# Batch 0 of a block-sorted attention kernel: the weighted values written transposed, with row sums from a product with ones

## The chip, the cores and the metric

The kernel runs on one core of one Trainium2 chip. The metric is the device time of one launch in microseconds. The kernel before takes 232.64 us (median of three runs, 232.14 to 233.84); the profiled execution spans 229.3 us.

Five engines work side by side, each in the order of its own queue: TensorE (PE, matrix products), VectorE (DVE), ScalarE (ACT), GpSimd (POOL, here mostly the issuer of loads that change the type) and SyncE (SP, the issuer of the other transfers). Products land in PSUM, which DVE and ACT empty into SBUF.

## What is computed

Attention over blocks that a soft permutation has sorted, and then a two-layer feed-forward network:

```python
for _ in range(5):                       # P = sort_net: 4 x 8 heads, 8 x 8 blocks
    P = exp(P - max(P)); P /= sum(P, -1) + 1e-9; P /= sum(P, -2) + 1e-9
k_sorted = einsum('bhij,bhjcd->bhicd', P, k_blocks)      # and the same for v
scores = scale * q_block @ k_sorted_block.T              # per block of 96 tokens
attn = exp(scores - max); attn /= sum(attn, -1)
x = attn @ v_sorted_block                                # (4 * 768) x (8 heads * 64)
h = maximum(x @ w_in, 0)                                 # w_in 512 x 2048
out = (s * h * h + b) @ w_out                            # w_out 2048 x 512
```

There are 4 batches, 8 heads, 768 tokens in 8 blocks of 96, and 64 numbers per head.

## The kernel before

**Stages.** The five softmax rounds of `sort_net` (lines 191 to 208) run at the start on DVE and ACT, while TensorE works on products of zeros (`warm`, line 156: the first argument is how many, the second how many columns each). From there each batch goes through the same pieces: `k_piece` and `v_piece` sort the keys and values by products with the permutation, `q_piece` or `q_blocks` transpose the queries, `s_piece` or `s_banks` make the scores of four blocks and a pair of heads and ACT takes their exponentials into a tile `at`, and the weighted values follow.

**Batches and halves.** A batch is cut into two halves of four blocks (384 tokens). `hp` counts the four pairs of heads. `ffn1(t, ...)` is the first layer for half `t` (0 to 7): eight steps `i`, each of 8 products of 128x384 into a two-bank PSUM tile, a ReLU on ACT (`rt`) and a square on DVE (`gt`). `ffn2(t, ...)` is the second layer. Both take a dictionary of slots: small pieces of other work that are put into the queues after step `i` (or, with the key `("pre", i)`, between the products and the ReLU of step `i`). `ahead=3` means that the products of head pairs 0 and 1 are issued for the first three steps before the other two pairs are needed; the keys -3 to -1 are slots between these.

**Weighted values, batch 0.** `p_piece(b, half, hp)` (line 345) uses the exponentials as the weights of the array, so that the result has tokens on its partitions: `pv`, 96 tokens x (8 groups of 64 values and a sum). The sum is a column of ones that stands beside the values in `VS`. DVE takes the reciprocal of 96x8 sums (line 361) and multiplies (line 362) into `x`. The feed-forward layer needs `x` transposed: for batch 0 `t_piece` (line 367) does it on TensorE in PSUM for two head pairs at a time and has DVE or ACT copy the result to `XT`; for batches 1 to 3 a DMA does it (`t_dma`).

**Buffers.** The PSUM pool `psa` has three buffers of two banks, which rotate over k, v, score, `pv` and first-layer tiles in the order of issue; `psb` has two of one bank. A piece that takes a buffer waits until the work that last used it is done.

**Order.** The queues follow the program's order; nothing is reordered. All loads with a change of type go through POOL's queue in its order: k of batch 0 in three parts, q blocks 0 to 3, then, held back by a small copy on POOL (line 464) that waits for the second key piece, `load_w`: w_in in 14 parts with q blocks 4 to 7 among them, and w_out in 4. `sum_w` and `make_bias` (column sums of w_out, for the term with `b`) lie in slots of `ffn1(1)`.

The order around the change, from line 471 on and in `ffn1(0)` and `ffn1(1)`, is written out by hand:

```python
s_piece(0, 0, 0); s_piece(0, 0, 1); p_piece(0, 0, 0)
s_piece(0, 0, 2); warm(1); p_piece(0, 0, 1)
s_piece(0, 0, 3); warm(1); p_piece(0, 0, 2); warm(1)
t_piece(0, 0, 0, "A"); p_piece(0, 0, 3)
```

Of the kernel before, what the change touches and what calls it, by code (L numbers as in the profile page):

```python
# [9 lines left out]
FP = mybir.dt.float32  # L10
BF = mybir.dt.bfloat16
AF = mybir.ActivationFunctionType
ALU = mybir.AluOpType
# [9 lines left out]
def kernel(  # L23
# [24 lines left out]
    C2 = BLK // 2  # L48
    GAP = 64
    KR = GAP + C2  # L50
    NG = NHP * NB
# [7 lines left out]
    const = ctx.enter_context(tc.tile_pool(name="const", bufs=1))  # L59
# [7 lines left out]
    osb = ctx.enter_context(tc.tile_pool(name="osb", bufs=3))  # L67
    psa = ctx.enter_context(tc.tile_pool(name="psa", bufs=3, space=bass.MemoryType.PSUM))
# [49 lines left out]
    nc.gpsimd.affine_select(out=emat, in_=emat, pattern=[[-H, B], [-1, H], [0, 2 * NB]], base=0,  # L118
                            channel_multiplier=1, compare_op=ALU.not_equal, fill=1.0)
    load("k", 0, 3)  # L120
    load_q(0, range(HB))
    ones = const.tile([128, 32], BF)
    wi = const.tile([128, NHP, d_ff], BF)
    wo = const.tile([128, NF, d_model], BF)
# [1 line left out]
    def load_w():  # L126
        wiv = moe_w_in.rearrange("(a p) f -> p a f", p=128)
        fq = d_ff // 4

        def part(a, f0, f1):  # L130
            nc.gpsimd.dma_start(out=wi[:, a, f0 * fq:f1 * fq], in_=wiv[:, a, f0 * fq:f1 * fq])  # L131

        for a in (0, 1):
            part(a, 0, 2)
        for a in (2, 3):
            part(a, 0, 1)
        load_q(0, range(HB, NB))
        for a in (2, 3):
            part(a, 1, 2)
        for c in (2, 3):  # L140
            for a in range(NHP):
                part(a, c, c + 1)
        wov = moe_w_out.rearrange("(f p) n -> p f n", p=128)
        for c in range(4):
            fs = slice(c * (NF // 4), (c + 1) * (NF // 4))
            nc.gpsimd.dma_start(out=wo[:, fs, :], in_=wov[:, fs, :])  # L146

    def fill_vs(i):
        nc.gpsimd.memset(VS[i][:, :, D:VW], 1.0)
        nc.gpsimd.memset(VS[i][32:GAP, :, D:VW], 0.0)  # L150
        nc.gpsimd.memset(VS[i][32:C2, :, D:VW], 1.0)

    fill_vs(0)
    Z = []

    def warm(n, w=512):
        for _ in range(n):
            if not Z:
                Z.append(psb.tile([128, 512], FP, tag="b", name="z"))
            nc.tensor.matmul(out=Z[0][:, 0:w], lhsT=zeros[:, 0:128], rhs=zeros[:, 0:w],  # L160
                             start=True, stop=True)
# [23 lines left out]
    nc.vector.tensor_tensor(out=sn, in0=sn, in1=rstat.broadcast_to([BH, NB, NB]),  # L185
                            op=ALU.subtract)
    warm(96, 32)
    warm(6)
    warm(122, 64)
    warm(8)  # L190
    for it in range(5):
        nc.scalar.activation(out=sn, in_=sn, func=AF.Exp)
        if it >= 1:
# [49 lines left out]
    def evac(eng, out, in_):  # L243
        if eng == "A":
            nc.scalar.copy(out=out, in_=in_)  # L245
        else:
            nc.vector.tensor_copy(out=out, in_=in_)  # L247
# [63 lines left out]
    AT = {}  # L311
    X = {}
# [51 lines left out]
            in0=pvv[:, :, :, 0:D],  # L364
            in1=rec.unsqueeze(3).broadcast_to([BLK, 2, HB, D]), op=ALU.mult)

    def t_piece(b, half, hp2, eng):

        x = X[b, half]
        if hp2 == 0:  # L370
            XT[b * 2 + half] = xtp.tile([128, HB, NHP, BLK], BF, tag="xt", name="xt")
        tr = psb.tile([128, 1024], BF, tag="b", name="tr")
        for hp in (hp2, hp2 + 1):
            for n in range(HB):
                c0 = (n * 2 + hp % 2) * BLK
                nc.tensor.transpose(out=tr[:, c0:c0 + BLK],
                                    in_=x[:, n, hp * 128:(hp + 1) * 128],
                                    identity=ident[0:BLK, 0:BLK])
        evac(eng, XT[b * 2 + half][:, :, hp2:hp2 + 2, :],
             tr[:, 0:2 * TG].rearrange("p (n a c) -> p n a c", n=HB, a=2))  # L380

    def t_dma(b, half):
        x = X.pop((b, half))
# [87 lines left out]
    v_piece(0, 3 * CK, "D")  # L471
    s_piece(0, 0, 0)
    s_piece(0, 0, 1)
    p_piece(0, 0, 0)
    s_piece(0, 0, 2)
    warm(1)
    p_piece(0, 0, 1)
    s_piece(0, 0, 3)
    warm(1)
    p_piece(0, 0, 2)  # L480
    warm(1)
    Z.clear()
    t_piece(0, 0, 0, "A")
    p_piece(0, 0, 3)

    s_bc = const.tile([128, 1], FP)
    b_bc = const.tile([128, 1], FP)
# [46 lines left out]
    def SC(b, h, i): return lambda: s_piece(b, h, i)  # L534
    def SB(b, h, i): return lambda: s_banks(b, h, i)
    def P(b, h, i): return lambda: p_piece(b, h, i)
    def TP(b, h, i, eng): return lambda: t_piece(b, h, i, eng)
    def TD(b, h): return lambda: t_dma(b, h)
    def PDB(b): return lambda: build_pd(b)
    def QB(b, n0, eng): return lambda: q_blocks(b, n0, eng)  # L540


    ffn1(0, {-2: [TP(0, 0, 2, "D")], ("pre", 1): [QB(0, HB, "D"), QB(0, HB + 2, "D")],
             2: [SB(0, 1, 0)], 3: [SB(0, 1, 1), P(0, 1, 0)], 4: [SB(0, 1, 2), P(0, 1, 1)],
             5: [SB(0, 1, 3), P(0, 1, 2)], 6: [TP(0, 1, 0, "D"), P(0, 1, 3)]}, ahead=3)
    ffn1(1, {-2: [TP(0, 1, 2, "D")], 1: [lambda: take_p(1, B - 1, PB), PDB(1)], 4: [PDB(2)],
             3: [sum_w], 5: [PDB(3), make_bias]}, ahead=3)
    gate = const.tile([128, 1], BF)

    def gated_loads(b):  # L550
# [56 lines left out]
```

The softmax here doesn't subtract the row's maximum and nothing guards it: scores larger than these inputs give would overflow.

## Time and profile before

| stretch, us | what runs | TensorE busy, us | VectorE busy, us |
|---|---|---|---|
| 20.0 to 26.4 | weighted values of half 0, first products of `ffn1(0)` | 4.68 of 6.40 | 4.61 |
| 26.4 to 42.05 | `ffn1(0)` with half 1's scores and weighted values in its slots | 14.98 of 15.65 | 9.44 |
| 42.05 to 53.86 | the rest of `ffn1(1)` | 11.20 of 11.81 | 5.50 |
| 53.86 to 229 | second layer of batch 0, and batches 1 to 3 | 169.08 of 175.14 | 92.65 |

The ends are landmarks of the trace: at 26.4 the last transposed quarter pair of half 0 is in `XT`, at 42.05 that of half 1, at 53.86 the second layer's first product starts. Over the whole span TensorE is busy 218.0 us (95%), DVE 125.3 us (55%), ACT 99.1 us (43%), POOL 67.2 us (29%). "Busy" of TensorE counts products whose modelled ends overlap, so it isn't a measure of how near its peak it runs.

### The profile page before, as it was taken

Reading aid. Unit: us, or ns where it says so; the run is one execution under the profiler, and the core shown is the slowest. Engines: PE = TensorE matmul, PEld = TensorE weight load, DVE = VectorE, ACT = ScalarE, POOL = GpSimd, SP = SyncE. Lnnn points to the kernel's source line nnn. Section 1 sums busy time; section 2 is a strip of 40 time slices with the busy share of each in tenths; the row PEclk is TensorE's granted clock in tenths of the full one; section 3 lists DMA queues with packets and bytes.
Section 4 is the critical chain, followed back from the end, with each engine's and each line's share of the span. In section 5 each row is a group of like instructions: output and inputs, shape, how many; then the busy total and the mean of one; then the engine's idle time right before and its main releaser. Section 6 shows DMA issues by size and latency. Waiting matters only on the chain.

```text
span 229.3 us, 5991 instructions
## 1 busy us (share of the span) xinstructions
PE 218.0 (95%) x2625; PEld 132.0 (58%) x2648; DVE 125.3 (55%) x223; ACT 99.1 (43%) x127; POOL 67.2 (29%) x110
## 2 busy tenths in 40 slices
PE   7997889999899999999999999999999999999993
PEld 5875646545656555666555556555555555654452
DVE  6757466552557544388647634499647534341221
ACT  4957366553433416646334226627152246650000
POOL 8419499344900008392000018291000000000000
PEclk9999999999999999999999999999999999999999
DMA  5997999999991566995111659993112340001212
GB/s 196 211 84 101 167 151 185 211 215 164 103 162 49 117 159 110 189 139 114 51 46 53 149 123 164 175 144 71 49 71 65 121 114 0 3 1 46 93 46 92
DMA packets 53642, 25.82 MB, mean 113 GB/s; under 512 B 44912, under 2 KB 48752, under 8 KB 53616
## 3 DMA queue, kind: packets, MB, share of 16 engines
q0 software_dynamic: 30576, 12.85, 46.4%
q1 hardware_dynamic: 23040, 12.59, 23.4%
q8 instruction: 20, 0.33, 0.6%
q14 instruction: 6, 0.05, 0.1%
HBM read 27.27 MB, written 6.29 MB: 146 GB/s over the span
## 4 chain that ended last, share of the span: by engine, by line
PE 79%; DMA 10%; DVE 4%; POOL 3%; issue 2%; ACT 1%; ACTq 0%; POOLq 0%
PE ops L429 33%; PE hps L404 27%; DMA wo<-in_moe_w_out_dram 6%; PE z L160 5%; DMA qtok<-in_q_dram 4%; DVE gt L419 3%; PE tv L306 3%; PE tp L256 3%; PE pv L356 3%; PE sc L321 2%; POOL wi L131 2%; PE ops L442 2%; POOL wo L146 1%; ACT rt L418 1%; DVE ks L247 1%
## 5 line engine op out<-in xcount | busy, mean ns | idle before, releaser
L404 PE MATMUL hps<-xt,wi 128*128 128x384 bf16 x512 | 85.9, 326 | 1.3 <-ACT xt L245 0.6
L429 PE MATMUL ops<-wo,gt 128*128 128x512 bf16 x348 | 81.4, 379 | 2.3 <-issue 1.9
L418 ACT ACTIVATE rt<-hps 128x768 bf16<-128x768 f32 x64 | 51.1, 811 | 56.9 <-PE hps L404 48.3
L419 DVE TENSOR_TENSOR gt<-rt 128x768 bf16<-128x768 bf16 x64 | 47.6, 750 | 43.7 <-ACT rt L418 42.9
L404 PEld LDWEIGHTS <-wi 128*128 128x128 bf16 x512 | 49.4, 98 | 34.9 <-DMA wi<-in_moe_w_in_dram 1.7
L429 PEld LDWEIGHTS <-gt 128*128 128x128 bf16 x368 | 33.6, 98 | 36.5
L450 DVE SCALAR_TENSOR_TENSOR ot<-ops,s_bc,bias 128x512 f32<-128x512 f32 (+1 forms) x25 | 18.2, 729 | 30.6 <-PE ops L429 28.3
L326 ACT ACTIVATE at<-sc 112x768 bf16<-112x768 f32 x28 | 21.3, 808 | 29.9 <-PE sc L321 29.9
L99 POOL DMA_DIRECT2D qtok<-in_q_dram x32 | 24.9, 791 | 19.3 <-DMA rawv<-in_v_dram 7.8
L362 DVE TENSOR_TENSOR x<-pv,rec 96x512 bf16<-96x512 f32 x32 | 22.0, 687 | 1.1
L247 DVE CAST vs<-tv 112x1024 bf16<-112x1024 f32 x11 | 13.3, 1223 | 10.8 <-PE tv L306 10.7
L170 POOL COPY vp<-rawv 128x384 bf16<-128x384 bf16 x24 | 19.1, 848 | 0.0
L356 PEld LDWEIGHTS <-at 112*128 112x128 bf16 (+1 forms) x256 | 12.8, 101 | 7.2 <-ACT at L326 1.1
L553 POOL COPY gate<-gt 128x1 bf16<-128x1 bf16 x2 | 0.4, 192 | 55.6 <-DVE gt L419 55.6
L356 PE MATMUL pv<-vs,at 112*128 112x66 bf16 (+1 forms) x256 | 13.9, 195 | 1.1 <-DVE vs L247 1.0
L160 PE MATMUL z<-zeros 128*128 128x64 bf16 (+2 forms) x235 | 12.3, 213 | 1.3 <-DVE zeros L102 1.0
L306 PEld LDWEIGHTS <-vp 128*64 128x64 bf16 x512 | 9.1, 113 | 3.9 <-issue 3.3
L306 PE MATMUL tv<-pd,vp 128*64 128x64 bf16 x512 | 10.2, 197 | 0.9 <-issue 0.7
L160 PEld LDWEIGHTS <-zeros 128*128 128x128 bf16 x238 | 8.6, 104 | 3.7 <-issue 1.7
L245 ACT CAST ks<-tp 128x1024 bf16<-128x1024 f32 x8 | 8.0, 1018 | 3.9 <-PE tp L256 3.9
L245 ACT CAST vs<-tv 112x1024 bf16<-112x1024 f32 x5 | 5.1, 1019 | 9.9 <-PE tv L306 9.9
L361 DVE RECIPROCAL rec<-pv 96x8 f32<-96x8 f32 x32 | 6.4, 200 | 4.9 <-PE pv L356 4.9
(77 smaller groups left out, 105.8 us busy)
## 6 DMA issues: line engine op xcount, KB each, us to landing
out_dram<-ot SPq DMA_DIRECT2D x23, 256.0 KB, 2.0
qtok<-in_q_dram POOLq DMA_DIRECT2D x32, 96.0 KB, 9.5
rawk<-in_k_dram POOLq DMA_DIRECT2D x3, 768.0 KB, 7.9
rawv<-in_v_dram POOLq DMA_DIRECT2D x3, 768.0 KB, 10.8
wo<-in_moe_w_out_dram POOLq DMA_DIRECT2D x4, 512.0 KB, 11.3
v0f<-in_v_dram SPq DMA_DIRECT2D x4, 384.0 KB, 4.8
wi<-in_moe_w_in_dram POOLq DMA_DIRECT2D x12, 128.0 KB, 5.8
rawk<-in_k_dram POOLq DMA_DIRECT2D x3, 256.0 KB, 8.1
```

The lines of the kernel that those rows point to most:

```text
L99: nc.gpsimd.dma_start(out=QTOK[b][:, n], in_=qv[:, n])
L160: nc.tensor.matmul(out=Z[0][:, 0:w], lhsT=zeros[:, 0:128], rhs=zeros[:, 0:w], start=True, stop=True)
L170: eng.tensor_copy(out=o, in_=i)
L306: nc.tensor.matmul(out=ps[z * GAP:(z + 1) * GAP, d, :], lhsT=VP[b % 2][:, d0 + d, :], rhs=PD[b][:, :, z, :], start=True, stop=True)
L326: nc.scalar.activation(out=at, in_=sc[0:KR, :, 0:TG], func=AF.Exp, scale=scale)
L356: nc.tensor.matmul(out=pv[0:m, e, n * VW:(n + 1) * VW], lhsT=atf[:, c0:c0 + m], rhs=VS[b % 2][:, e * NG + g0 + n, :], start=True, stop=True)
L362: nc.vector.tensor_tensor(out=x[:, :, hp * 128:(hp + 1) * 128].rearrange("p n (e d) -> p e n d", e=2), in0=pvv[:, :, :, 0:D], in1=rec.unsq ...
L404: nc.tensor.matmul(out=H1[i][:, f, 0:TG], lhsT=wi[:, hp, fc:fc + 128], rhs=xt[:, :, hp, :], start=(hp == 0), stop=(hp == NHP - 1))
L418: nc.scalar.activation(out=rt, in_=h, func=AF.Relu)
L419: nc.vector.tensor_tensor(out=gt[:, 2 * i:2 * i + 2, :], in0=rt, in1=rt, op=ALU.mult)
L429: nc.tensor.matmul(out=ops, lhsT=gt[:, f, m * 128:(m + 1) * 128], rhs=wo[:, f, :], start=(f == 0), stop=(f == NF - 1))
L450: nc.vector.scalar_tensor_tensor(out=ot[:, ns], in0=ops, scalar=s_bc, in1=BIAS[0][:, ns], op0=ALU.mult, op1=ALU.add)
```

## The change

For batch 0 the weighted values come out already transposed. `pt_piece` takes the place of `p_piece` and `t_piece`: the sorted values are the weights of the array and the exponentials stream past them, so the result has the 128 numbers of a head pair on its partitions and 384 tokens along the row, as `XT` wants it. The sums over keys are then needed on every one of the 128 partitions: two more products, with a matrix of ones (`rsum`, with zeros in the rows of the gap) in the place of the values, write them as a tile `ps` of 128x384. DVE takes the reciprocal of that tile into `rec` and multiplies it with `pv` into `XT`. The transposes, their copies and the tile `x` fall away for batch 0.

Beside that: the w_in loads of the first half of its columns go in quarters (512 columns each) for all four row groups, in place of two halves and four quarters; q blocks 4 and 5 are loaded with 0 to 3, ahead of the copy that holds back `load_w`, and 6 and 7 stay in it; three products of zeros between the pieces go, and the ones of the start are 3 wide, 125 narrow and 10 wide in place of 6, 122 and 8; `ffn1(1)` no longer issues its products ahead; `sum_w` moves from step 3 to step 5 and `make_bias` from 5 to 7.

```diff
-    load_q(0, range(HB))
+    load_q(0, range(HB + 2))
...
-        for a in (0, 1):
-            part(a, 0, 2)
-        for a in (2, 3):
-            part(a, 0, 1)
-        load_q(0, range(HB, NB))
-        for a in (2, 3):
-            part(a, 1, 2)
+        for c in (0, 1):
+            for a in (0, 1):
+                part(a, c, c + 1)
+        for c in (0, 1):
+            for a in (2, 3):
+                part(a, c, c + 1)
+            if c == 0:
+                load_q(0, range(HB + 2, NB))
...
+    rsum = const.tile([KR, D], BF)
+    nc.gpsimd.memset(rsum, 1.0)
+    nc.gpsimd.memset(rsum[32:GAP], 0.0)
+    nc.gpsimd.memset(rsum[32:C2], 1.0)
...
-    warm(6)
-    warm(122, 64)
-    warm(8)
+    warm(3)
+    warm(125, 64)
+    warm(10)
...
-    def t_piece(b, half, hp2, eng):
...
+    def pt_piece(b, half, hp, own=False):
+        g0 = hp * NB + half * HB
+        at = AT.pop((b, half, hp))
+        if hp == 0:
+            XT[b * 2 + half] = xtp.tile([128, HB, NHP, BLK], BF, tag="xt", name="xt")
+        if own:
+            pv, ps = [psb.tile([128, TG], FP, tag="b", name="ptb") for _ in range(2)]
+        else:
+            pt = psa.tile([128, 2, 512], FP, tag="a", name="pt")
+            pv, ps = pt[:, 0, 0:TG], pt[:, 1, 0:TG]
+        for n in range(HB):
+            for e in range(2):
+                nc.tensor.matmul(out=pv[e * 64:(e + 1) * 64, n * BLK:(n + 1) * BLK],
+                                 lhsT=VS[b % 2][:, e * NG + g0 + n, 0:D],
+                                 rhs=at[:, e, n * BLK:(n + 1) * BLK], start=True, stop=True)
+        for e in range(2):
+            nc.tensor.matmul(out=ps[e * 64:(e + 1) * 64, :], lhsT=rsum, rhs=at[:, e, :],
+                             start=True, stop=True)
+        rec = osb.tile([128, d_model], FP, tag="ot", name="rect")[:, 0:TG]
+        nc.vector.reciprocal(out=rec, in_=ps)
+        nc.vector.tensor_tensor(out=XT[b * 2 + half][:, :, hp, :],
+                                in0=pv.rearrange("p (n t) -> p n t", n=HB),
+                                in1=rec.rearrange("p (n t) -> p n t", n=HB), op=ALU.mult)
...
-    p_piece(0, 0, 0)
+    pt_piece(0, 0, 0)
     s_piece(0, 0, 2)
     warm(1)
-    p_piece(0, 0, 1)
+    pt_piece(0, 0, 1)
     s_piece(0, 0, 3)
-    warm(1)
-    p_piece(0, 0, 2)
-    warm(1)
     Z.clear()
-    t_piece(0, 0, 0, "A")
-    p_piece(0, 0, 3)
+    pt_piece(0, 0, 2)
...
-    ffn1(0, {-2: [TP(0, 0, 2, "D")], ("pre", 1): [QB(0, HB, "D"), QB(0, HB + 2, "D")],
-             2: [SB(0, 1, 0)], 3: [SB(0, 1, 1), P(0, 1, 0)], 4: [SB(0, 1, 2), P(0, 1, 1)],
-             5: [SB(0, 1, 3), P(0, 1, 2)], 6: [TP(0, 1, 0, "D"), P(0, 1, 3)]}, ahead=3)
-    ffn1(1, {-2: [TP(0, 1, 2, "D")], 1: [lambda: take_p(1, B - 1, PB), PDB(1)], 4: [PDB(2)],
-             3: [sum_w], 5: [PDB(3), make_bias]}, ahead=3)
+    ffn1(0, {-2: [PTP(0, 0, 3, True)],
+             ("pre", 1): [QB(0, HB, "D"), QB(0, HB + 2, "D")],
+             2: [SB(0, 1, 0)], 3: [SB(0, 1, 1), PTP(0, 1, 0)], 4: [SB(0, 1, 2), PTP(0, 1, 1)],
+             5: [SB(0, 1, 3), PTP(0, 1, 2)], 6: [PTP(0, 1, 3)]}, ahead=3)
+    ffn1(1, {1: [lambda: take_p(1, B - 1, PB), PDB(1)], 4: [PDB(2)], 5: [PDB(3), sum_w],
+             7: [make_bias]})
```

More of the change, by code (lines that the diff above doesn't have):

```diff
@@ L365, in p_piece @@
             in1=rec.unsqueeze(3).broadcast_to([BLK, 2, HB, D]), op=ALU.mult)
-    def t_piece(b, half, hp2, eng):
-        x = X[b, half]
-        if hp2 == 0:
+    def pt_piece(b, half, hp, own=False):
+        g0 = hp * NB + half * HB
+        at = AT.pop((b, half, hp))
+        if hp == 0:
             XT[b * 2 + half] = xtp.tile([128, HB, NHP, BLK], BF, tag="xt", name="xt")
[L372 to L380, printed above, removed]
+        if own:
[16 more added lines that the diff above has]
+                                in1=rec.rearrange("p (n t) -> p n t", n=HB), op=ALU.mult)
     def t_dma(b, half):
@@ L536, in P, with PTP @@
     def P(b, h, i): return lambda: p_piece(b, h, i)
-    def TP(b, h, i, eng): return lambda: t_piece(b, h, i, eng)
+    def PTP(b, h, i, own=False): return lambda: pt_piece(b, h, i, own)
     def TD(b, h): return lambda: t_dma(b, h)
```

## The prediction

> **What bounds the kernel now.** I read the page's busy shares first, then the chain of work that ended last, then the shapes on VectorE, then the timeline of 20 to 54 us, where all the edits lie.
>
> ```profile
> PE 218.0 (95%) x2625; PEld 132.0 (58%) x2648; DVE 125.3 (55%) x223; ACT 99.1 (43%) x127; POOL 67.2 (29%) x110
> ...
> PE 79%; DMA 10%; DVE 4%; POOL 3%; issue 2%; ACT 1%; ACTq 0%; POOLq 0%
> ```
>
> TensorE sets the time; VectorE holds 4% of the chain. But these are averages. The chain in order of time shows that the start is another regime:
>
> ```profile
> 10.31 1.67 PE z L160 x7
> 11.99 1.03 PE pe L219 x8
> ...
> 19.72 8.14 DMA qtok<-in_q_dram
> 27.86 0.28 issue
> ...
> 33.06 14.14 DMA wo<-in_moe_w_out_dram
> 47.21 0.04 issue
> ...
> 53.86 2.54 PE ops L429 x11
> ```
>
> Products of zeros hold up the permutation at 11.99; then come the q and w_out loads; from 53.86 on nearly all is TensorE. So 53.86 (the first second-layer product) is the landmark: what follows is 175 us of work that the change doesn't touch, and moves as one piece.
>
> VectorE's forms, with the time of one:
>
> ```profile
> L450 DVE SCALAR_TENSOR_TENSOR ot<-ops,s_bc,bias 128x512 f32<-128x512 f32 x23 | 17.3, 751 | 28.3 <-PE ops L429 28.3
> L362 DVE TENSOR_TENSOR x<-pv,rec 96x512 bf16<-96x512 f32 x32 | 22.0, 687 | 1.1
> L361 DVE RECIPROCAL rec<-pv 96x8 f32<-96x8 f32 x32 | 6.4, 200 | 4.9 <-PE pv L356 4.9
> ...
> L450 DVE SCALAR_TENSOR_TENSOR ot<-ops,s_bc,bias 128x256 f32<-128x256 f32 x2 | 1.0, 484 | 2.3 <-PE ops L442 2.3
> L198 DVE RECIPROCAL rrec<-rstat 32x8 f32<-32x8 f32 x5 | 1.0, 191 | 0.2
> ...
> L233 DVE RECIPROCAL RC<-cs 128x3 f32<-128x3 f32 x1 | 0.2, 176 | 0.0
> L233 DVE RECIPROCAL RC<-cs 128x1 f32<-128x1 f32 x1 | 0.2, 165 | 0.0
> ```
>
> An ordinary operation costs (751-484)/256 = 1.04 ns for each element of a row. The reciprocal is dearer: from 1 to 3 elements on 128 partitions it grows by 11 ns, 5.5 ns each; from 3 to the 8 of L361, 24 ns, 4.8 each. Today its rows are 8 long, so this is hidden in the fixed 160 ns. The change makes them 384 long.
>
> **What the Trainium skill says.** "VectorE: DVE Perf Modes", section "First, the fixed hardware budget": the reciprocal is an iterative divide with a repeat count of 8, unlike the one-slice operations. The trace agrees that it is several times dearer per element, but shows about 5 cycles at the page's 0.96 GHz, not 8. The same page, "Why PSUM operands drop a tier": fp32 from PSUM runs at one element a cycle; the 1.04 ns agree. "TensorE: Matmul & The Clock Gate", section "What's actually happening": TensorE runs at half rate until it has been busy for a window of about 3.4 us, and falls back after an idle one. The trace agrees at the start: weight loads of the first wide zero products stand 0.43 us apart, the last seven take 0.24 each.
>
> **The change part by part.**
>
> *Reciprocal.* 160 + 384 x 5.4 = 2.23 us, once for each of 8 pieces. Bounds: 0.56 us if long rows ran at 1.04 ns; 1.3 to 1.6 if the slope were 3.0 (128x3 to 32x8) or 3.7 (128x1 to 32x8), which mix partition counts; 0.15 + 384 x 8/0.96 = 3.36 us, an estimate from the page's repeat count. I take 2.23, since 128x1, 128x3 and 96x8 lie on one line.
>
> *Multiply.* 128x384 from PSUM: 687 - 128 x 1.04 = 0.55 us. With gaps of 0.03 between VectorE instructions a piece costs it 2.84 us. Before, it costs 0.20 + 0.69 us and half a copy of 0.55 (one of the four copies is ACT's): 8 x 0.89 + 3 x 0.55 = 8.8 us in all. After: 22.7. VectorE gains 13.9 us of work, mostly between 20 and 42, where it has 6.40-4.61 + 15.65-9.44 = 8.0 us idle. That alone forces about 6 us; the order of dependences adds to it.
>
> *TensorE.* Removed: 8 x 0.43 (L356) and 4 x 0.51 (transposes) = 5.5 us. Added: per piece 8 products of 96 columns (as a score piece, 0.34) and two of 384 (0.16 each) = 0.66, so 5.3. Nothing either way.
>
> *Half 0.* The first weighted values come at 20.8, the first reciprocal at about 21.5 (0.25 later than the 21.25 of before, for the longer piece). VectorE then runs the four pieces back to back: 21.5 + 4 x 2.84 = 32.9 for head pair 3 of half 0. Before, this stands at 26.37:
>
> ```profile
> 25.81 0.56 DVE L247 COPY xt<-tr 128x768 bf16<-128x768 bf16 x1 [0.84 <-PE tr L376]
> 27.76 1.51 ACT L418 ACTIVATE rt<-hps 128x768 bf16<-128x768 f32 x2 [3.19 <-PE hps L404]
> ```
>
> The fourth score piece also waits for the first multiply, which frees its PSUM buffer (24.3, before 22.24), but its exponential (done by 25.7) is ready well ahead of its turn on VectorE. First-layer products of pairs 0 and 1 for three steps (2 us) go in the meantime; then TensorE stands until 32.9. First ReLU at 33.5, 5.7 later. The q blocks and w_in that before arrive at 28 to 30 are then long there.
>
> *Half 1.* In steps 3 to 6 VectorE has to do a square (0.56), a reciprocal and a multiply in each: 3.43 us with gaps. TensorE's pace before is 1.95:
>
> ```profile
> 32.86 1.47 PE L404 MATMUL hps<-xt,wi 128*128 128x384 bf16 x8
> ...
> 34.81 1.47 PE L404 MATMUL hps<-xt,wi 128*128 128x384 bf16 x8
> ...
> 36.77 1.47 PE L404 MATMUL hps<-xt,wi 128*128 128x384 bf16 x8
> ```
>
> Three PSUM buffers rotate between first-layer tiles and pieces, so step i+2 waits for the multiply of the piece of step i: TensorE falls to VectorE's pace. From 33.5, steps 0 to 3 with the q blocks take till 38.8 (before: 27.76 to 33.7, part of it a wait for w_in that is now gone). Then 38.8 + 2.84 + 3 x 3.43 = 51.9 for the last multiply into half 1's `XT`. Before: 42.05.
>
> *`ffn1(1)`.* Its first step needs all four pairs, so no product beyond the first three gets past 51.9; the missing `ahead` costs little beside that. Then 61 products at 20.80/128 = 0.1625 us (a later stretch of the chain) = 9.9, the sums of w_out 16 products in 1.1, the bias 0.86: 63.8, against 53.86. All of w_out is there by 47.2 in the trace of before, so the wait of 0.85 us inside those sums is gone, and moving them later costs nothing. Sum so far: +9.9.
>
> *Zeros at the start.* Three wide ones at 0.43 fewer, two more at 0.24, three more narrow ones; the clock turns at about 7 us in both (narrow ones 36 ns each before it, 21 after): 5.25 + 49 x 0.036 + 76 x 0.021 + 10 x 0.24 = 11.0 in place of 11.98. The permutation is ready at 11.07, so its products go 0.75 us earlier than 11.91, and so does all of the above. -0.75.
>
> *Loads.* The two q blocks follow q 0 to 3 in a gap (32 GB/s in 14 to 16 us, 8 in 16 to 18), w_in's first quarters come a little sooner: hidden behind VectorE now. The three fills of `rsum` on POOL lie in its 8 us of waiting before line 464. Batch 1's k and v loads have 9 us more, so TensorE's wait for the value copy on POOL (0.42 at 60.66) goes: about -0.4. The dropped three zero products lie in what is now idle.
>
> Sum: 232.64 + 9.9 - 0.75 - 0.4 = **241.4 us**.
>
> **The rivals.**
> A. *Long rows at full rate* (0.56 us): a piece costs VectorE 1.17, half 0 is ready near 26.7, half 1 near 41.2, no load is waited for, and the second layer starts about 1 us sooner; with the zeros and POOL's wait, 230.5. For it: the removed transposes and waits for q and w_in (1.4 and 1.7 us of POOL, 0.6 and 1.7 of TensorE). Against: three sizes show 5 ns an element.
> B. *A middle slope* (1.3 to 1.6 us): half 1 ready at 44.6 to 46.5, second layer at 56.5 to 58: +2.6 to +4.1, less 1.15: 234 to 235.6. For it: the 32x8 form at 191. Against: it has 32 partitions; a sum over 64 elements takes 207 ns there and 220 on 128.
> C. *Eight cycles an element*, 3.36 us: half 1 at 61, second layer at 73, 250.5. For it: the page's count. Against: 8.3 ns would put 128x3 at 182, not 176.
> D. *TensorE goes cold* in the idle of 22 to 33 us: its products slow to half for a few us. For it: it works about half of that time and stands 2 us at once. Against: no gap reaches 3.4 us, and VectorE, not it, is awaited. Up to +2 on the forecast: 243.5.
>
> **How the numbers follow.** Forecast with D's share: 0.72; A 0.10; B 0.10; C 0.08. The forecast's own spread: slope 5 to 6 ns gives reciprocals of 2.08 to 2.46, that is about -1.2 and +1.8 (eight of them, nearly all exposed), and D to 245 on top. Range 235 to 245.5: holds the forecast and the upper end of B, leaves out A, C and the rest of B. Faster is A, 0.10; slower the forecast, C and nearly all of B, 0.88; same 0.02.
>
> **What would show it.** Right: reciprocals of 128x384 near 2.2 us, 18 us in all; VectorE nearly full from 21 to 52; the chain in that stretch on the reciprocal line, not q and w_out loads; first-layer products waiting for VectorE; the second layer's first product at about 63; the stretch after it as long as before. Wrong: reciprocals under 1 us (A), or a wait of TensorE for loads before 50.

## The result: 14 us slower, and the profile after

The changed kernel takes 247.08 us (median of four runs, 245.12 to 251.60) against 233.02 us of the kernel before; the ratio is 1.0576, 95% interval 1.0491 to 1.0662. The direction and the main mechanism, VectorE's long reciprocals, were forecast (241.4 us, range 235 to 245.5), but the time lies above the range. One thing has to be known to read the times below: the granted TensorE clock differs from run to run of one kernel (0.945 to 0.970 over these four), a run in which it falls longer takes longer, and the ratios leave out runs more than 1.5% above the fastest.

The page of the changed kernel, busy shares and chain by engine, then the granted clock in 40 slices of 6.1 us each; the last line is the clock of the kernel before, in slices of 5.7 us:

```profile
PE 225.4 (93%) x2632; PEld 132.7 (55%) x2632; DVE 143.2 (59%) x220; ACT 98.5 (40%) x126; POOL 69.4 (29%) x115
...
PE 85%; DVE 12%; ACT 1%; issue 1%
...
PEclk9999579997999999999999999999999999999999
```

```profile
PEclk9999999999999999999999999999999999999999
```

VectorE has 17.9 us more to do (143.2 against 125.3) and holds 12% of the chain against 4%. The waits for q and w_out are gone from the chain. New is the fall of the clock: before, the row is all nines; here it is lower in slices 5, 6 and 10.

The chain of waits of the changed kernel in order of time (start, length, what) shows where the 14 us are:

```profile
18.52 0.94 issue
...
21.62 2.57 DVE rect L393
...
24.21 0.56 DVE xt L394
24.77 2.48 DVE rect L393
...
33.38 0.57 DVE xt L394
...
33.99 2.18 PE hps L420 x7
36.17 1.28 PE tqb L293 x16
...
50.95 0.56 DVE xt L394
51.50 0.47 DVE gt L435
51.97 2.48 DVE rect L393
...
54.47 0.57 DVE xt L394
...
55.08 8.97 PE hps L420 x45
64.05 0.98 PE cps L534 x16
```

From 21.62 to 33.95 and from 40.83 to 55.04 the chain runs through VectorE: reciprocal, multiply, next reciprocal, and in half 1 a square between. Between the halves it runs for 6.0 us through TensorE (first-layer products, the q transposes and a score piece) and 0.8 through a ReLU. The last multiply ends at 55.03, where before the last copy into half 1's `XT` ended at 42.05; the second layer begins at 68.43, before at 53.86. The two lines of the timelines, the copy before and the second layer's first products after:

```profile
41.50 0.55 DVE L247 COPY xt<-tr 128x768 bf16<-128x768 bf16 x1
```

```profile
68.43 2.75 PE L445 MATMUL ops<-wo,gt 128*128 128x512 bf16 x12
```

After that nothing has changed: 243.3 - 68.43 = 174.9 us to the end, before 229.3 - 53.86 = 175.4.

VectorE's two new forms (count, busy us, mean ns):

```profile
L393 DVE RECIPROCAL rect<-pt 128x384 f32<-128x384 f32 x7 | 17.9, 2551 | 0.6 <-PE pt L390 0.6
...
L394 DVE TENSOR_TENSOR xt<-pt,rect 128x384 bf16<-128x384 f32 x7 | 3.9, 557 | 0.2
L393 DVE RECIPROCAL rect<-ptb 128x384 f32<-128x384 f32 x1 | 2.5, 2548 | 0.0
```

The multiply is the 0.55 us of the forecast. The reciprocal is 2.55 us, not 2.23.

The stages of the kernels below are compared by these landmarks, read in each timeline (us):

| kernel | first reciprocal of batch 0's values | last write into half 1's `XT` ends | second layer begins | from there to the end |
|---|---|---|---|---|
| before | 21.25 | 42.05 | 53.86 | 175.4 |
| after | 21.62 | 55.03 | 68.43 | 174.9 |
| forecast for after | 20.75 | 51.15 | 63.05 | 175.0 |
| e2_busy | 22.38 | 55.69 | 70.41 | 174.5 |
| e10_form (copies) | | 40.09 | 51.99 | 174.9 |
| e13_after (after again) | 24.29 | 57.61 | 72.37 | 174.7 |
| e14_same (TensorE kept busy) | 24.37 | 56.99 | 68.90 | 174.9 |
| e15_stream (before, short stream) | 20.25 | 40.55 | 52.00 | 175.4 |
| e16_stream_after | 21.92 | 54.16 | 68.92 | 174.9 |
| e17_stream_busy | 20.13 | 52.74 | 64.64 | 174.5 |

The forecast's row takes its 0.75 us for the zero products off its 21.5, 51.9 and 63.8. The last column is the same for all to 0.9 us: nearly all that differs lies before it.

### The profile page after: what moved, and what is told of

Same layout as the page of the kernel before. It is cut to its first block, busy times and chain, and to the rows that moved or that the text cites. A ratio compares the mean times of both kernels' runs of the same rounds, so it can differ in the third digit from the quotient of the medians.

```text
span 243.3 us, 5981 instructions
## 1 busy us (share of the span) xinstructions
PE 225.4 (93%) x2632; PEld 132.7 (55%) x2632; DVE 143.2 (59%) x220; ACT 98.5 (40%) x126; POOL 69.4 (29%) x115
## 3 DMA queue, kind: packets, MB, share of 16 engines
HBM read 27.27 MB, written 6.29 MB: 138 GB/s over the span
## 4 chain that ended last, share of the span: by engine, by line
PE 85%; DVE 12%; ACT 1%; issue 1%
PE ops L445 33%; PE hps L420 32%; DVE rect L393 8%; PE z L165 5%; PE tv L311 4%; PE pv L361 3%; PE tp L261 2%; PE sc L326 2%; DVE xt L394 2%; PE ops L458 1%; DVE gt L435 1%; PE tqb L293 1%; DVE vs L252 1%; PE pe L224 0%; ACT ks L250 0%
## 5 line engine op out<-in xcount | busy, mean ns | idle before, releaser
L420 PE MATMUL hps<-xt,wi 128*128 128x384 bf16 x512 | 89.9, 335 | 9.5 <-DVE xt L394 8.3
L445 PE MATMUL ops<-wo,gt 128*128 128x512 bf16 x368 | 85.7, 380 | 0.0
L420 PEld LDWEIGHTS <-wi 128*128 128x128 bf16 x512 | 50.5, 100 | 46.9 <-issue 15.6
L435 DVE TENSOR_TENSOR gt<-rt 128x768 bf16<-128x768 bf16 x64 | 49.0, 774 | 40.0 <-ACT rt L434 39.4
L175 POOL COPY vp<-rawv 128x384 bf16<-128x384 bf16 x24 | 19.9, 881 | 0.0
L393 DVE RECIPROCAL rect<-pt 128x384 f32<-128x384 f32 x7 | 17.9, 2551 | 0.6 <-PE pt L390 0.6
L367 DVE TENSOR_TENSOR x<-pv,rec 96x512 bf16<-96x512 f32 x24 | 16.5, 686 | 0.8
L361 PEld LDWEIGHTS <-at 112*128 112x128 bf16 x192 | 9.9, 101 | 5.7
L361 PE MATMUL pv<-vs,at 112*128 112x66 bf16 x192 | 10.4, 195 | 0.0
L131 POOL DMA_DIRECT2D wi<-in_moe_w_in_dram x16 | 8.6, 553 | 2.6 <-DMA wi<-in_moe_w_in_dram 1.8
```

Of the source, the lines that this page charges most:

```text
L175: eng.tensor_copy(out=o, in_=i)
L361: nc.tensor.matmul(out=pv[0:m, e, n * VW:(n + 1) * VW], lhsT=atf[:, c0:c0 + m], rhs=VS[b % 2][:, e * NG + g0 + n, :], start=True, stop=True)
L393: nc.vector.reciprocal(out=rec, in_=ps)
L420: nc.tensor.matmul(out=H1[i][:, f, 0:TG], lhsT=wi[:, hp, fc:fc + 128], rhs=xt[:, :, hp, :], start=(hp == 0), stop=(hp == NHP - 1))
L435: nc.vector.tensor_tensor(out=gt[:, 2 * i:2 * i + 2, :], in0=rt, in1=rt, op=ALU.mult)
L445: nc.tensor.matmul(out=ops, lhsT=gt[:, f, m * 128:(m + 1) * 128], rhs=wo[:, f, :], start=(f == 0), stop=(f == NF - 1))
```

## Experiments

### Is it the reciprocal?

**e1_copy.** A copy in its place.

```diff
-        nc.vector.reciprocal(out=rec, in_=ps)
+        nc.vector.tensor_copy(out=rec, in_=ps)
```

> The changed kernel with the eight reciprocals of 128x384 turned into plain copies of the sums, so the weighted values are multiplied by their sums and not divided: this part of the computation is left out. A copy of 128x384 fp32 from PSUM should take 0.55 us against the 2.55 us that the reciprocal takes in the profile after. Theory (the long-row reciprocals on VectorE are the cause, and TensorE's lowered clock follows from the idle that they make): eight times 2.0 us leave VectorE, half 0 is ready near 26.5, half 1 near 41.5, the granted clock is back at 0.99 or more, and the whole takes 230 to 234 us. Rival (the missing products ahead of the second half, the other form of the products and the new order of loads carry a good part): it stays at 237 to 243 us.

Measured: 234.21 us, ratio to before 1.0103 (1.0041 to 1.0165), granted clock 0.976 to 0.991. Copies took 0.55 us each. So 4.7 of the 5.8% hang on the length of that one instruction, as the theory has it (6.6 of 7.6 with the changed kernel's later ratio, e13_after); but the clock did not come back, and 234.21 is just above the theory's range. Something besides the reciprocal was left: in its profile the first copy began at 24.88, behind two waits in TensorE's stream of 2.13 and 1.20 us, which are taken up below.

**e3_recip.** The other direction: the kernel before, with an idle reciprocal added to each of the eight pieces (`bias` is filled with ones early, and gets its value later as ever).

```diff
         nc.vector.reciprocal(out=rec, in_=pvv[:, :, :, D])
+        if b == 0:
+            nc.vector.reciprocal(out=bias[:, 0:TG], in_=bias[:, 0:TG])
```

> The kernel before with one idle reciprocal of 128x384 fp32 (on a constant in SBUF) put between the small reciprocal and the multiply of each of the eight weighted-values pieces of batch 0; nothing else changes. Theory (VectorE's added time alone makes the loss): each takes 2.5 us, a piece costs VectorE 3.4 us, half 0 is ready about 10 us later and half 1's pieces come every 4 us in place of 2: 243 to 249 us, as slow as the changed kernel or slower. Rival (VectorE has 8 us to spare between 20 and 42 us and the pieces are not awaited at once): 233 to 238 us.

Measured: 248.30 us, ratio 1.0757 (1.0695 to 1.0819), clock 0.950 to 0.965. None of the change's other parts is in it, and it is as slow as the change. The rival, room on VectorE, falls.

**e9_half.** Half of the columns.

```diff
-        nc.vector.reciprocal(out=rec, in_=ps)
+        nc.vector.reciprocal(out=rec[:, 0:TG // 2], in_=ps[:, 0:TG // 2])
...
-                                in1=rec.rearrange("p (n t) -> p n t", n=HB), op=ALU.mult)
+            in1=spread(rec, [[0, 2], [BLK, 2], [1, BLK]]), op=ALU.mult)
```

> The changed kernel with the reciprocal taken of half of the columns only: 128x192 in place of 128x384, used twice, so that the second half of the tokens is divided by the sums of the first: this part of the computation is changed. By the measured sizes it takes 1.35 us in place of 2.55. Theory (the reciprocals are exposed nearly whole, and the loss is linear in their length): eight times 1.2 us less, 9.6 us, and a little more from the clock: about 237 to 239 us, close to the middle between the changed kernel (247) and the one with copies (234 on its chip, 3 us over the kernel before). Rival (the clock and TensorE's fetch waits carry most of it, so that it falls in a step and not in proportion): 241 us or more, or already at 234.

Measured: 236.68 us, ratio 1.0267 (1.0212 to 1.0322), clock 0.971 to 0.976. This is 0.3 us under the theory's range. The ratios of the three lengths (0.55, 1.35 and 2.55 us of VectorE) are 1.010, 1.027 and 1.058, but they come from different chips, and the changed kernel alone gave 1.058 and, repeated, 1.076 (e13_after). The profiles show the shape better. From the first reciprocal or copy to the last multiply it takes 18.8 us in e10_form (copies, below), 22.9 in e9 and 33.4 in the changed kernel: the first 8 x 0.8 = 6.4 us of VectorE's time cost 4.0, the next 9.6 cost 10.5, of which 1.2 are the clock between the halves. So there is no step, but a bend, not a line: the shorter pieces still find part of VectorE's idle time, and from half length on nearly all of it is exposed.

### Why was the reciprocal mis-sized?

**e5_sizes.** Many lengths, after the last store of the kernel before.

```diff
+    for parts in (128, 32):
+        for n in (1, 3, 8, 16, 48, 96, 192, 384):
+            nc.vector.reciprocal(out=w[0:parts, 0:n], in_=w[0:parts, 0:n])
...
+    for n in (8, 96, 384):
+        nc.vector.reciprocal(out=w[:, 0:n], in_=ps[:, 0, 0:n])
```

> The kernel before with reciprocals of many row lengths added after its last store: 1, 3, 8, 16, 48, 96, 192 and 384 fp32 elements on 128 and on 32 partitions in SBUF, and 8, 96 and 384 on 128 partitions from PSUM. Theory (the cost is a fixed part and one slope over all lengths, and the forecast's 5.4 ns an element was read too low from rows of 1 to 8): the slope is (2551 - 165)/383 = 6.2 ns at 96 and more, the same on 32 and 128 partitions and from PSUM and SBUF. Rival (the slope of short rows, 5.4 ns, is right there, and PSUM or the partition count makes long rows dearer): 384 in SBUF takes 2.2 us.

Its VectorE groups by shape; the mean time of one in ns stands after the comma:

```profile
L585 DVE RECIPROCAL bias<-psx 128x384 f32<-128x384 f32 x1 | 2.6, 2557 | 0.0
L581 DVE RECIPROCAL bias<-bias 128x384 f32<-128x384 f32 x1 | 2.6, 2553 | 0.0
L581 DVE RECIPROCAL bias<-bias 32x384 f32<-32x384 f32 x1 | 2.5, 2541 | 0.0
...
L581 DVE RECIPROCAL bias<-bias 128x96 f32<-128x96 f32 x1 | 0.8, 753 | 0.0
...
L581 DVE RECIPROCAL bias<-bias 128x16 f32<-128x16 f32 x1 | 0.3, 253 | 0.0
...
L581 DVE RECIPROCAL bias<-bias 128x8 f32<-128x8 f32 x1 | 0.2, 203 | 0.0
...
L581 DVE RECIPROCAL bias<-bias 128x3 f32<-128x3 f32 x1 | 0.2, 175 | 0.0
```

From 8 elements on the slope is (2553-203)/376 = 6.25 ns; from 3 to 8 it is (203-175)/5 = 5.6. 128 partitions in place of 32 add 12 ns from 3 elements on, and PSUM 3 to 4, whatever the length. Theory: right. The forecast's 5.4 came from rows too short to show the slope, and mixed 96 with 128 partitions. Its rival C, eight cycles, would be 8.3 ns; at the 0.96 GHz that the Trainium skill gives ("VectorE: DVE Perf Modes", section "Specifications") 6.25 ns are six.

### What the small parts of the change do

**e4_small** put all of them into the kernel before; **e6_sixq** the q blocks alone, **e7_zeros** the zero products alone, **e11_rest** all but the q blocks. **e8_fourq** took the q blocks out of the changed kernel.

```diff
e4, e6         -    load_q(0, range(HB))
e4, e6         +    load_q(0, range(HB + 2))
e4, e7, e11    -    warm(6)
e4, e7, e11    -    warm(122, 64)
e4, e7, e11    -    warm(8)
e4, e7, e11    +    warm(3)
e4, e7, e11    +    warm(125, 64)
e4, e7, e11    +    warm(10)
e4, e11        w_in in quarters; sum_w in step 5, make_bias in step 7
e8             -    load_q(0, range(HB + 2))
e8             +    load_q(0, range(HB))
```

> The kernel before with only the small parts of the change: six q blocks ahead of the held-back loads, w_in in quarters, 3 wide, 125 narrow and 10 wide zero products at the start, column sums in step 5 and the bias in step 7 of the second half. The weighted values stay as they were, and so do the products issued ahead. Theory (these parts are neutral or help a little): TensorE no longer waits for q and w_in at 28 to 30 us, 231 to 232.5 us. Rival (in the changed kernel a part of the loss comes from them): 234 to 236 us.

> The kernel before with only the q blocks moved: six in place of four ahead of the held-back loads, two within them. Theory (the two more blocks keep the transfer engines full to about 15.3 us in place of 14.2, and TensorE's instruction fetches, which lie in the same stretch, come late: in the kernel with the small parts together TensorE stood 1.65 us at 15.5 and 2.13 us at 20.1 for nothing that the profile shows): two such waits of 1 to 2 us here too, a lower clock after them, 233.5 to 236 us. Rival (the other small parts, above all the zero products, bring the waits and the clock): 230.5 to 232 us, as before.

> The kernel before with only the zero products of the start changed: 3 wide, 125 narrow and 10 wide. Theory (they are shorter by 0.2 to 0.8 us and leave the clock as it is): 230 to 231.5 us. Rival (fewer wide products at the start leave the clock nearer to falling, and it falls between 20 and 34 us): 233 us or more, with a granted clock under 0.99.

> The kernel before with the small parts except the q blocks: w_in in quarters, the shorter zero products, sums in steps 5 and 7. Theory (each is neutral or helps, and only the q blocks did harm): 229.5 to 230.8 us, a little under the kernel before. Rival (the quarters, with two more loads in the held-back series, also delay something): 231.5 us or more.

> The changed kernel with four q blocks ahead of the held-back loads, as in the kernel before, and four within them; the rest of the change stays. Theory (the late instruction fetches belong to the two q blocks and cost the changed kernel 1 to 3 us): 243 to 245.5 us against 247, the first long reciprocal at 21.2 us or sooner. Rival (VectorE's reciprocals hide whatever TensorE loses ahead of them, or the fetches have nothing to do with q): 246 to 248 us.

Measured: e4 235.55 us, ratio 1.0160 (1.0106 to 1.0214), where the theory had 231 to 232.5; e6 235.64 us, of which three runs took 235.2 to 238.3 at a clock of 0.964 to 0.978 (the ratio of 1.0234, 1.0111 to 1.0356, is that of these three) and one 230.1 at a clock of 1.0, no more than the kernel before; e7 230.97 us, 0.9975 (0.9948 to 1.0001); e11 231.15 us, 1.0025 (1.0002 to 1.0048); e8 247.64 us, 1.0632 (1.0463 to 1.0801).

The rest of the small parts is neutral, and e11's expected gain did not show. With the two q blocks ahead a run at a lower clock is likelier in the kernel before: a clock of 0.985 or less stood in all six runs of e4 and three of four of e6, against five of 20 in e7 and four of 22 in e11. Those are few runs, and where the clock holds no loss is shown. In the changed kernel taking the q blocks back helped nothing. So they are not the cause of the mishap; at most they make it likelier.

The mishap itself is a wait in TensorE's timeline. First e4_small, then the kernel before, the products of the value pieces (in brackets the idle time ahead and what ended it):

```profile
15.15 0.35 PE L307 MATMUL tv<-pd,vp 128*64 128x64 bf16 x10
17.14 1.04 PE L307 MATMUL tv<-pd,vp 128*64 128x64 bf16 x54 [1.65 <-issue]
...
19.00 1.11 PE L307 MATMUL tv<-pd,vp 128*64 128x64 bf16 x58
22.24 0.28 PE L307 MATMUL tv<-pd,vp 128*64 128x64 bf16 x6 [2.13 <-issue]
```

```profile
17.63 1.14 PE L306 MATMUL tv<-pd,vp 128*64 128x64 bf16 x60
19.12 0.25 PE L306 MATMUL tv<-pd,vp 128*64 128x64 bf16 x4 [0.35 <-issue]
```

"issue" is time in which nothing that the profile shows was awaited. Sixteen profiles have that start with its narrow products. In twelve there is a wait at both places, 10 to 12 products into the first value piece and 4 to 6 before the end of the fourth; in the other four (both of the first comparison, e3 and e10) only the second. They last 0.35 to 2.7 us: 0.94 us in the first profile of the changed kernel, and 4.5 us in two parts in that of e8. What they bring about is seen in e4: the window of 3.4 us with the second wait has TensorE busy for only 1.2 us, and from 23.1 us on the clock is half for 10.2 us.

**e15_stream.** Do the waits belong to the work, or to the place in the stream of instructions?

```diff
     warm(6)
-    warm(122, 64)
+    warm(12)
     warm(8)
```

> The kernel before with the 122 narrow zero products of the start replaced by 12 wide ones, which take about as long: 110 products and as many weight loads fewer ahead of the key and value pieces, and nothing else. TensorE's two waits for nothing that the profile shows stand at the 11th product of the first value piece and near the end of the fourth in every kernel so far. Theory (they belong to places in TensorE's instruction stream, where the next stretch of instructions is fetched, and not to the work there): both move about 110 products later, the first into the fourth value piece, the second beyond the scores into the first layer, and the runs vary less. Rival (they belong to the work or to the time, such as buffers or the transfers of q): they stay at the same products or the same microseconds.

Measured: 229.48 us, ratio 0.9955 (0.9936 to 0.9973), the 22 runs between 228.32 and 230.72 us at a clock of 0.991 to 1.0. Its value products:

```profile
14.91 1.42 PE L306 MATMUL tv<-pd,vp 128*64 128x64 bf16 x64
...
17.05 1.32 PE L306 MATMUL tv<-pd,vp 128*64 128x64 bf16 x64
```

Both waits are gone from the value pieces, and the first reciprocal comes at 20.25. They did not turn up 110 products later either, so neither theory nor rival came out as written.

Two things in the kept traces settle what the waits are. First, their places are counted in products: with 6 + 122 + 8 = 136 zero products ahead they stand 12 products into the first piece and 4 before the end, with 3 + 125 + 10 = 138 two products earlier (10 and 6), and from one to the other there are 128 products, each with its weight load (52 + 16 + 60 or 54 + 16 + 58). Second, the DMA part of the page has a queue of kind "instruction" with 20 packets, and in the packed traces these are 16384 bytes each. All 28 waits in the value pieces end 1.25 to 1.62 us after the end of one of these packets; in e4 they end at 15.88 and 20.71, and TensorE goes on at 17.14 and 22.24. So these are late fetches of instructions.

In e15 the packet ends at 16.32. By the count, the place that it serves lies 110 products later, near 17.9 us (an estimate from the count and the 1.32 us of the last 64 products): 1.6 us after the packet, and no wait is left. Twelve wide products take about as long as 122 narrow ones but are far fewer instructions. What makes a packet come late stays open: the second one starts between 13.0 and 15.4 us in these sixteen profiles, with four q blocks (e11, 15.4) as with six (the changed kernel, 13.0). This version is 0.45% under the kernel before.

### What the clock costs

**e2_busy** and **e12_allbusy** give TensorE something to do where it stands for VectorE: e2 repeats products of two pieces, e12 also puts wide zero products ahead of the third first-layer tile and of the second half.

```diff
e2, e12   -    pt_piece(0, 0, 2)
e2, e12   +    pt_piece(0, 0, 2, times=5)
e2, e12   -    ffn1(0, {-2: [PTP(0, 0, 3, True)],
e2, e12   +    ffn1(0, {-2: [PTP(0, 0, 3, True, 3)],
...
e12       +            if t == 0 and i == ahead - 1:
e12       +                H1[i] = psa.tile([128, 2, 512], FP, tag="a", name="hps")
e12       +                for _ in range(12):
e12       +                    nc.tensor.matmul(out=H1[i][:, 0, :], lhsT=zeros[:, 0:128],
e12       +                                     rhs=zeros, start=True, stop=True)
...
e12       +             7: [Z.clear, lambda: warm(16)]}, ahead=3)
```

> The changed kernel with the products of the third weighted-values piece issued five times and those of the fourth three times, each time with the same result in the same place, so that TensorE works in the time in which it stood from 24.8 to 27.9 and from 29 to 31 us. Theory (the lowered clock between 24 and 36 us is an effect of its own, which costs the seven products of 2.18 us at 34 us and the sixteen transposes of 1.28 us about 1.7 us): these run at full rate, the second layer starts 1.5 to 2 us earlier, 243 to 245.5 us against 247. Rival (the clock is not set by this idle, or VectorE is awaited in any case): 246 to 249 us with the same granted clock.

> The changed kernel with TensorE kept busy in all three places where it stood for VectorE: the repeated products of the third and fourth piece, twelve wide zero products ahead of the third first-layer tile (30 to 33 us), and sixteen ahead of the second half's first product (50 to 54 us). VectorE's work is the same. Theory (TensorE's lowered clock is a loss of its own only where TensorE is awaited, above all in the products after 55 us: 45 of them took 8.97 us and not 7.3): the granted clock is 0.985 or more, 243.5 to 245.5 us against 247. Rival (the clock costs nothing, since VectorE is awaited throughout): 247 us with the better clock too.

Measured: e2 248.43 us, 1.0719 (1.0657 to 1.0781). The clock held until 34.2 us, then was half to 37.6 and again from 54.7 to 61.5 us: the low stretches moved and the time did not gain. Here the theory failed. e12: 244.01 us, 1.0580 (1.0520 to 1.0639), with the same ratio as the first runs of the changed kernel, on another occasion: unclear. So both were put side by side, e14_same being the kernel of e12.

> The changed kernel itself again, on one chip with the kernel whose TensorE is kept busy. Theory (5 us of the loss beyond the forecast are the longer reciprocal, 2.6 us, the clock after 55 us, 1.5 us, and TensorE's waits near 15 and 20 us, which differ from run to run): 245 to 248 us, with a granted clock of 0.96 to 0.975. Rival (the first runs were an unlucky draw): 242 to 244 us.

> The changed kernel with TensorE kept busy while VectorE is awaited, now beside the changed kernel on one chip. Theory (the clock costs something of its own in the products after the last multiply): 1 to 2.5 us under the changed kernel, and the same 11.9 us from the end of the last multiply to the second layer where the changed kernel has 13.4. Rival (the clock's loss is hidden behind VectorE): less than 0.7 us apart.

Measured: e13 248.51 us, ratio 1.0760 (1.0701 to 1.0818); e14 246.75 us (one run of 241.66 at a clock of 0.998, five of 245.5 to 247.2 at 0.971 to 0.979; no ratio). So one and the same kernel gave 1.0576 and 1.0760 on two occasions, and ratios of different experiments can be held against each other to about 2% only. The repeated run of the changed kernel was slower than the first: its first reciprocal came at 24.29. The medians differ by 1.8 us; plainer is the landmark: from the last multiply to the second layer 14.8 us in e13 and 11.9 in e14. The theory's 13.4 for the changed kernel was that of its first profile; the clock takes different stretches in different runs. e14's own first reciprocal is late for the same reason as e13's, waits of 2.25 and 0.56 us in the stream.

The last pair took the waits in the stream away from the changed kernel (e16), and the idle of TensorE too (e17).

```diff
e16, e17  -    warm(125, 64)
e16, e17  +    warm(13)
e17       and the edits of e12
```

> The changed kernel with its 125 narrow zero products of the start replaced by 13 wide ones, so that the stream ahead of the key and value pieces is 112 products shorter, as in the kernel that did away with TensorE's waits near 15 and 20 us. Theory (these waits cost the changed kernel what its first long reciprocal comes late: 24.29 us in its second profile, 21.62 in its first, against 20.6 without them): first reciprocal at 20.6, last multiply ended 33.4 later at 54.0, second layer 13.4 later at 67.4, and 174.7 to the end: a span of 242 and a time of 243.5 to 244.5 us, with less spread. Rival (VectorE's chain or the clock takes back what the start gains): 246 us or more.

> The same stream, and TensorE kept busy in the three places where it stands for VectorE. Theory (with the waits of the start gone and the clock kept, only the reciprocals are left of the loss): second layer 11.9 us after the last multiply and not 13.4, 241.5 to 243 us, granted clock 0.99 or more, at least 1 us under the kernel with the shorter stream alone. Rival (the clock is hidden behind VectorE): the two within 0.7 us.

Measured: e16 243.87 us, ratio 1.0538 (1.0473 to 1.0602); e17 241.21 us, 1.0452 (1.0403 to 1.0502), clock 0.986 to 1.0. The last stretch of e17's chain, to be held against the changed kernel's (8.97 us for the same 45 products):

```profile
52.18 0.57 DVE xt L395
52.75 0.04 issue
52.79 7.47 PE hps L421 x45
60.26 0.98 PE cps L540 x16
61.24 2.71 PE hps L421 x16
```

7.47 and not 8.97 us: 1.5 us of the changed kernel's loss in its first profile are clock, where TensorE is awaited; in e13 the same 45 products took 10.33, 2.9 us more than in e17. Between e16 and e17 lie 2.7 us of the medians, more than the 1 us that the theory asked for.

e16's time is as expected; its first reciprocal, expected at 20.6, came at 21.92 in the execution profiled, the slowest of the six, and e17's at 20.13. No wait in the stream made it late: ScalarE, in the order of its queue, stood 1.97 us for a load of v until 10.64, and with it the last softmax round that the permutation needs. So a late load at the start is one more thing that differs from run to run.

### Is the new form worth anything?

**e10_form.** The new form with a cheap stand-in for the reciprocal and none of the small load and zero-product parts (the order of w_in and the zero products go back too; not printed).

```diff
-    load_q(0, range(HB + 2))
+    load_q(0, range(HB))
...
-        nc.vector.reciprocal(out=rec, in_=ps)
+        nc.vector.tensor_copy(out=rec, in_=ps)
```

> The kernel before with only the new form of the weighted values (transposed, the product with ones, no products ahead in the second half, sums in steps 5 and 7), the reciprocal turned into a copy (that part of the computation is left out), and the q blocks, the order of w_in and the zero products as before. Theory (the form with a cheap reciprocal would be worth 1 to 2 us, and what held the kernel with copies at 234 us were the q blocks and what they do to TensorE's fetches and clock): 229 to 231 us. Rival (the form is worth nothing even with a free reciprocal): 231.5 to 234 us.

Measured: 230.17 us, ratio 0.9961 (0.9936 to 0.9986). With a division that cost no more than a copy the form would gain 0.4%. In the profiled execution, the fastest of the 20, the second layer begins at 51.99, 1.9 us earlier than in the first profile of the kernel before.

## Why the prediction was right, and where it was wrong

Its working, against the first profile of the changed kernel, whose span of 243.3 us is 5.25 over the forecast's 229.3 + 8.75 = 238.05:

- **Reciprocal (the step that failed first).** "160 + 384 x 5.4 = 2.23 us" measured 2.55: the slope is 6.25 ns, and the spread given, 2.08 to 2.46, did not reach it. The three sizes that it calls one line (165, 176 and 200 ns at 1, 3 and 8 elements) give 5.0 from end to end, still further off. Of the 8 x 0.32 = 2.6 us some was given back, since a reciprocal starts about 0.08 us before the recorded end of the multiply ahead, where 0.03 of gap was assumed. A piece of half 0 costs 3.06 us, not 2.84 (multiplies at 24.21 and 27.27), one of half 1 3.52, not 3.43 (43.90 and 47.42). Half 0 took 12.3 us (forecast 11.4), half 1's four pieces 13.7 (13.1): 1.5 us more.
- **Rival D, the cold clock (the second step that failed).** It was given up to 2 us, with "no gap reaches 3.4 us, and VectorE, not it, is awaited" against it, and no share of the forecast's sum. The clock fell without such a gap, and TensorE is awaited twice. Between the halves (33.94 to 41.31 us on VectorE) 7.4 us passed where 5.9 were forecast; seven products took 2.18 us in place of 1.14, the q transposes 1.28 in place of 0.69. With the clock at full there (e8, e9, e16) it is 6.2: 1.2 us are clock, and 0.3 the forecast's own. After 55 us, 45 products took 8.97 us, 7.47 in e17: 1.5 us.
- **Zeros at the start (the third).** "-0.75" did not come: the permutation's products began at 11.69 in place of 11.91, 0.2 earlier (0.5 in e13), and a wait in the stream of 0.94 us stood ahead of the scores. The first reciprocal came at 21.62, not 20.75: 0.9 us. In e13 it came at 24.29.
- Together 0.9 at the start, 1.5 for the reciprocal, 1.2 and 1.5 for the clock, 0.3 between the halves, -0.1 at the end: 5.3 us, all of the 5.25. The median lies 2 us over this profile's run; in e13, slower still, the waits and the clock were worse. e17, with neither on its path, has a span of 239.1, 1 us over the forecast's, and a ratio of 1.0452 where 241.4 against 232.64 would be 1.038.
- **Loads.** Hidden behind VectorE, as said: the chain has none of them. What no term holds is that TensorE's own instructions are loads too, and come late in this stretch. Whether the extra q blocks add to that is not shown: low-clock runs were more frequent with them in the kernel before (e4, e6), but e8, without them, had the longest waits of the changed kernel's form, 4.5 us together.
- **TensorE's products, `rsum`'s fills, the lost `ahead`:** nothing, as said. The stretch from last multiply to second layer was forecast at 63.8 - 51.9 = 11.9; it is 11.9 in e14 and e17, where the clock held. The 0.4 us at batch 1's values came too (174.9 against 175.4), but by luck: the 0.42 us at 60.66 is a wait of weight loads, ahead of which TensorE's products run on without a break. What went is a wait of 0.39 us in the stream, at 61.83 in the kernel before, which ended 1.25 us after an instruction packet. The 0.85 us inside the sums of w_out is one of weight loads too; the products waited 0.56. And the change drops two zero products between the pieces, not three; the one that stays (21.79, 0.39 us) is not waited for.
- **The rivals.** A and B fall with the measured slope, C too. With the measured reciprocal, clock and start the same chain gives the profiled span, so the form of the argument stands. Two terms were mis-sized, and the clock was left out of the sum on an argument that did not hold.

## What to carry to other kernels

An operation that is cheap on eight numbers may be the dearest on 384: before a change lengthens an operation's rows, take its slope from sizes near the new one, and where only short rows are at hand, widen the range upwards. When VectorE becomes the bound, TensorE's idle is not free: its clock falls, and the price is paid later, where TensorE is awaited again. And ahead of a critical start a long stream of tiny filler products may be worse than a few wide ones that take as long, since instructions must be fetched: 12 in place of 122 made the kernel before 0.45% faster and its runs alike.

## What the runs showed of the hardware that was not expected

The clock. TensorE in windows of 3.41 us of the changed kernel, laid so that the changes of clock fall on their edges (busy us, then the mean granted clock):

```profile
17.20:20.61 3.41, 2.05 (x87) 1.00 0.70 86
20.61:24.02 3.41, 1.94 (x39) 1.00 1.06 137
24.02:27.43 3.41, 1.29 (x11) 0.50 1.65 179
27.43:30.85 3.42, 2.97 (x17) 0.50 1.22 182
30.85:34.26 3.41, 1.42 (x9) 1.00 1.00 141
34.26:37.67 3.41, 3.41 (x25) 0.50 1.24 206
...
51.32:54.74 3.42, 0.32 (x1) 1.00 2.33 152
54.74:58.15 3.41, 3.07 (x10) 0.50 1.52 118
```

Each window at half clock follows one in which TensorE was busy for 0.32 to 1.94 of 3.41 us, and each return follows one with 2.97 or more; after 2.05 the clock stayed. So a window that is somewhat more than half busy can already lose the clock for the next. This narrows what the Trainium skill says in "TensorE: Matmul & The Clock Gate", section "What's actually happening", which ties the fall to an idle window of about 3.4 us: the length agrees, the window need not be idle.

The other profiles agree. In each of the 19, windows of 3.413 us were laid on its own changes of clock, from 12 to 70 us. At full clock, all 19 windows with at most 1.63 us busy lost it for the next, all 244 with 2.11 or more kept it, and of the 13 between (1.91 to 2.07) four lost it. At half clock none of the 20 with at most 2.67 us came back, nine of 13 with 2.85 to 3.33 did, and all 14 that were full did. Outside that stretch three windows with 1.41 to 1.71 us kept the clock (e16, e11, e10), and "busy" holds modelled ends, so about 2 us is a measured border of these kernels, not an exact rule.

The instruction fetches are the other: TensorE stood 0.35 to 2.7 us at places that lie 128 products and 128 weight loads apart, each time until 1.25 to 1.62 us after a packet of 16384 bytes of its instruction queue had ended, and not at all with 110 products fewer ahead. Why the packets come late in some runs stays open.
